# A planned order set anew: attention and a gated feed-forward on one core, with traced task durations in the planner

## The chip, the cores and the metric

One Trainium2 chip, one core in use. The metric is the device time of one launch in microseconds (us), the median of several runs. A profiled execution of the same kernel gives the trace; its own time is told beside its span.

## The reference

Block-sparse attention of 4 batches, 8 heads, 768 positions, head size 64, in blocks of 32 positions, followed by a feed-forward over the 3072 tokens:

```python
scores = scale * np.matmul(q, k.transpose(0, 1, 3, 2))
mask = np.abs(blk_i - blk_j) <= 1
mask = mask | (blk_i == 0) | (blk_j == 0) | (blk_i == n_blocks - 1) | (blk_j == n_blocks - 1)
...
mask[qb * block:(qb + 1) * block, kb * block:(kb + 1) * block] = True    # 3 sampled blocks per query block
scores = np.where(mask, scores, -1000000000.0)
attn = np.exp(scores - np.max(scores, axis=-1, keepdims=True))
attn = attn / (np.sum(attn, axis=-1, keepdims=True) + 1e-09)
x = np.matmul(attn, v)                    # regrouped to 3072 tokens x 512
h = x @ w_in                              # 512 x 2048
g = h * np.tanh(np.log1p(np.exp(h)))      # for h over 20 the logarithm is h itself
out = g @ w_out                           # 2048 x 512
```

The inputs q, k, v are float32, the weights float64 (the kernel reads them as pairs of int32).

## The kernel before

**The work.** Each batch is 13 attention jobs: 11 pairs of query blocks (a gathered set of 8 key blocks for each) and two dense rows of blocks (the first and the last, all 768 keys). A job makes scores `s` on TensorE (L774 for batch 0, in float32; L784 for the others, in float16 high and low parts), row maxima `mx` on VectorE (L827), exponentials `pt` on ScalarE (L853), turns them round (in batch 0 by TensorE transposes `t`, L873, copied to `pp` by ScalarE or VectorE; later by a transposing DMA), multiplies with v into `o` (L938, L954), scales to `xs`, transposes to `tx` and splits into `xh` and `xl` (L1038, L1040, L1043). Eight query blocks make one tile of 256 tokens. A tile then goes through the feed-forward: 16 pieces of 12 matmuls for h (L1228, "H pieces" below), a chain of elementwise work on `hs` and `us` (L1237 to L1275), and 16 pieces of 6 matmuls for the output y (L1289, "Y pieces"). There are 12 tiles, so 192 pieces of each kind.

**The start.** The float64 weights must be decoded on VectorE (L1078, L1081, L1084: 8 pieces of w_in, 16 of w_out), scaled by a root of a Gram matrix that TensorE makes (L475, reduced through `tp`, L501), and split into high and low halves (`wt`, `wi`, `wo` on GpSimd, ScalarE or VectorE). Until that is done for the first pieces there is no H piece to run, and TensorE fills waits that the planner foresees with multiplications by zeros (L1057).

**What sets the order.** Nothing is ordered by hand. `Plan.add` records some thousands of tasks, each with one or more engines that can do it ("ways"), a planned duration on each, a latency `lat`, buffers of rings, and a number `K(name, n)` out of the table `PRIO`. `Plan.emit` walks a planned time: at each step it takes, over all engines, the task with the earliest planned start, and within 0.02 us the one with the least `ready + key`; a task with several ways goes to the engine where it is planned to end first. The instructions are written out in that order, and each engine runs its own in order on the chip:

```python
late, bias = pace(t, start) if eng == "PE" else (0.0, 0.0)
cand.append((start + late, t.ready + t.key + bias, t.n, start, t, took))
...
c = min((c[1:] for c in cand if c[0] <= lo + 0.02), key=lambda c: c[:2])
...
self.zeros(int((idle - 0.3) / (0.25 if start > 15.0 else 0.4)))
```

The last line puts zeros into a planned wait of TensorE, between 3 and 150 us of planned time. `pace` ranks attention jobs on TensorE by `START` (planned times for the first 18 jobs) and `RES` (how much feed-forward is kept back behind the last job). So a duration or a number in the table can move any task on any engine, and can give it to another engine.

**Two places the prediction speaks of.** `gather_k` (L698 on GpSimd, L700 on ScalarE) copies three sampled key blocks into `kg` for a query block. `sums` (L551, its instruction at L466) squares and adds a loaded tile on ScalarE; `add_root` has TensorE add the result over the partitions (`tp`), in order with everything else on TensorE.

Of the kernel before, what the change touches and what calls it, by code (L numbers as in the profile page):

```python
# [114 lines left out]
    "gh": (359.8, 691.9, 379.7, -99.7),  # L115
    "gl": (401.7, 134.8, 711.4, 354.1),
    "ys": (-152.2, 277.9, -237.6, -376.8),
    "out": (274.8, 328.6, 274.4, -199.6),
}


# [1392 lines left out]
```

## Time and profile before

| | us |
|---|---|
| median of 3 runs | 715.48 (714.74 to 716.0) |
| the profiled execution, its own time | 715.61 |
| its span, first to last instruction | 713.8 |
| TensorE busy | 677.6 |
| VectorE busy | 561.5 |
| ScalarE busy | 533.75 |
| GpSimd busy | 255.9 |

The engines are named PE (TensorE matmul), PEld (its weight loads), DVE (VectorE), ACT (ScalarE), POOL (GpSimd) and SP (the queue that issues the DMAs). "Busy" is the time in which at least one instruction of the engine ran; a group's mean is of single instructions, which overlap a little on their engine. Idle time of PE is what the span has over its busy time; the zeros are busy but do no work.

### The profile page before, as it was taken

How to read it: one execution, taken by the hardware profiler on the slowest of the kernel's cores; microseconds unless marked ns; L12 is line 12 of the kernel's file. 1: busy time of each engine (PE TensorE's matmuls, PEld its weight loads, DVE VectorE, ACT ScalarE, POOL GpSimd, SP SyncE). 2: the span in 40 equal slices, each digit the busy share in tenths (PEclk: the TensorE clock that was granted, in tenths of full speed). 3: DMA queues.
4: the chain of work that ended last, by engine and by line, in shares of the span. 5: the costliest groups of instructions: out<-in, count | busy, mean ns of one | idle time of the engine just before them, and what ended most of it. 6: DMA issues, size and time to landing. Idle time of an engine off the chain costs nothing.

```text
span 713.8 us, 25374 instructions
## 1 busy us (share of the span) xinstructions
PE 677.6 (95%) x10342; PEld 448.4 (63%) x10342; DVE 561.5 (79%) x1052; ACT 533.7 (75%) x908; POOL 255.9 (36%) x339
## 2 busy tenths in 40 slices
PE   6878898799999999999999999999999999999997
PEld 2544576566667666666666666666666666666653
DVE  2798988999899887899998979989979778554250
ACT  1868768898898876879887886998878868555550
POOL 6547534982233441262235325435212123000000
PEclk9999999999999999999999999999999999999999
DMA  8978794556556775588665775885495565530000
GB/s 321 362 218 264 249 286 116 141 169 123 168 137 164 197 201 129 151 202 205 147 157 138 214 200 120 227 218 138 119 165 126 129 144 145 143 89 16 16 16 29
DMA packets 144599, 115.93 MB, mean 162 GB/s; under 512 B 96739, under 2 KB 107492, under 8 KB 144484
## 3 DMA queue, kind: packets, MB, share of 16 engines
q1 hardware_dynamic: 144480, 114.33, 59.8%
q8 instruction: 81, 1.33, 0.8%
q14 instruction: 34, 0.28, 0.1%
q10 hardware_dynamic: 4, 0.00, 0.0%
HBM read 79.32 MB, written 12.95 MB: 129 GB/s over the span
## 4 chain that ended last, share of the span: by engine, by line
PE 61%; DVE 16%; DMA 9%; ACT 6%; issue 4%; SPq 2%; POOL 1%; ACTq 0%; POOLq 0%; DVEq 0%
PE y L1289 27%; PE h L1228 25%; PE s L784 4%; PE o L954 4%; DMA wor<-in_moe_w_out_dram 2%; DMA vg<-vd 2%; DMA wr<-in_moe_w_in_dram 2%; DVE p L904 2%; DMA raw_q<-in_q_dram 2%; DVE mx L827 1%; ACT pt L853 1%; DVE hs L1262 1%; DVE kt L613 1%; DVE wo L1084 1%; SPq L734 1%
## 5 line engine op out<-in xcount | busy, mean ns | idle before, releaser
L1228 PE MATMUL h<-xh,wi 128*128 128x256 f16 x1536 | 284.6, 274 | 0.3 <-ACT xh L1038 0.3
L1289 PE MATMUL y<-wo,g 128*128 128x512 f16 x1152 | 278.6, 380 | 1.3 <-DVE ys L1302 0.9
L1228 PEld LDWEIGHTS <-wi 128*128 128x128 f16 x2304 | 222.3, 98 | 60.3 <-issue 5.9
L1228 PE MATMUL h<-xl,wi 128*128 128x256 f16 x768 | 210.2, 274 | 0.7 <-POOL xl L1043 0.7
L1289 PEld LDWEIGHTS <-g 128*128 128x128 f16 x1152 | 109.5, 98 | 105.6 <-issue 7.0
L698 POOL COPY kg<-kt 128x256 f16 (+1 forms) x132 | 65.6, 534 | 137.0 <-PE s L784 113.3
L853 ACT ACTIVATE pt<-s,nb,ns 128x256 f32<-128x256 f32 (+1 forms) x208 | 106.8, 578 | 3.9 <-DVE p L904 3.4
L1237 ACT ACTIVATE hs<-h 128x512 f32<-128x512 f32 x96 | 56.5, 589 | 50.3 <-PE h L1228 49.6
L1262 DVE SCALAR_TENSOR_TENSOR hs<-us,hs 128x1024 f32<-128x1024 f32 x48 | 62.5, 1301 | 22.4 <-ACT us L1261 22.2
L1040 POOL CAST xh<-tx 128x256 f16<-128x256 f32 (+1 forms) x39 | 27.5, 712 | 120.0 <-DVE tx L1020 119.8
L904 DVE SCALAR_TENSOR_TENSOR p<-pt,p 128x512 f16<-128x512 f32 (+1 forms) x102 | 64.2, 651 | 2.4 <-ACT p L897 2.1
L827 DVE TENSOR_REDUCE mx<-s 128x4 f32<-128x1024 f32 x44 | 53.3, 1212 | 7.0 <-PE s L784 5.9
L700 ACT ACTIVATE kg<-kt 128x256 f16 (+1 forms) x132 | 40.8, 372 | 23.3 <-DMA kt<-in_k_dram 11.6
L1252 ACT ACTIVATE us<-hs,hsc 128x1024 f32<-128x1024 f32 x48 | 55.1, 1148 | 1.0
L1260 ACT ACTIVATE us<-us 128x1024 f32<-128x1024 f32 x48 | 50.6, 1054 | 6.8 <-POOL us L1258 6.2
L1259 ACT ACTIVATE us<-us 128x1024 f32<-128x1024 f32 x36 | 38.0, 1055 | 18.6 <-DVE us L1256 18.4
L1261 ACT ACTIVATE us<-us 128x1024 f32<-128x1024 f32 x48 | 50.6, 1054 | 0.7
L1256 DVE TENSOR_SCALAR us<-us 128x1024 f32<-128x1024 f32 x48 | 34.9, 726 | 18.3 <-ACT us L1252 18.3
L1273 POOL TENSOR_TENSOR g<-hs,g 128x1024 f16<-128x1024 f32 x15 | 34.4, 2291 | 34.1 <-DVE g L1270 25.6
L1043 POOL TENSOR_TENSOR xl<-tx,xh 128x128 f16<-128x128 f32 (+1 forms) x41 | 31.9, 785 | 39.3 <-ACT xh L1038 31.0
L1275 DVE TENSOR_TENSOR g<-hs,g 128x1024 f16<-128x1024 f32 x33 | 42.0, 1274 | 2.3 <-ACT g L1268 1.9
L954 PEld LDWEIGHTS <-pp 128*32 128x32 f16 x2952 | 32.4, 97 | 12.3 <-issue 10.6
(207 smaller groups left out, 909.4 us busy)
## 6 DMA issues: line engine op xcount, KB each, us to landing
vg<-vd SPq DMA_DIRECT2D x304, 65.0 KB, 2.4
vg<-vd SPq DMA_DIRECT2D x80, 195.0 KB, 3.3
wr<-in_moe_w_in_dram SPq DMA_DIRECT2D x8, 1024.0 KB, 11.3
wor<-in_moe_w_out_dram SPq DMA_DIRECT2D x16, 512.0 KB, 7.2
vd<-v SPq DMA_DIRECT2D x12, 520.0 KB, 5.4
raw_v<-in_v_dram SPq DMA_DIRECT2D x12, 512.0 KB, 4.8
out_dram<-ys SPq DMA_DIRECT2D x24, 256.0 KB, 3.2
raw_k<-in_k_dram SPq DMA_DIRECT2D x9, 512.0 KB, 5.7
```

The source lines that it names most:

```text
L698: nc.gpsimd.tensor_copy(out=dst, in_=src)
L827: nc.vector.tensor_reduce(out=mx.rearrange("p g w -> p (g w)"), in_=tl[ks].rearrange("p g (w k) -> p (g w) k", k=KT), axis=AX.X, op=ALU.max)
L853: ex = lambda o, x, g, w: nc.scalar.activation(out=o, in_=x, func=AF.Exp, bias=nb[:, g, w:w + 1], scale=ns(w)[:, 0:1])
L904: nc.vector.scalar_tensor_tensor(out=x[:, 1, cs], in0=src, scalar=PSC, in1=x[:, 0, cs], op0=ALU.mult, op1=ALU.subtract)
L954: nc.tensor.matmul(o[cs, at] if v1 == VW else o[cs, at, 0:v1 - v0], p[:, k, g, cs], x, start=j == 0 and g == 0 and k == 0 and n == 0, stop ...
L1228: nc.tensor.matmul(h[:, f2].rearrange("p (s q) -> p s q", q=BS), wi[:, fp, w, cc, fs], x[:, :, cc], start=f2 == 0 and k == 0, stop=f2 == 1 ...
L1237: nc.scalar.activation(out=tl[kq][:, 2 * (fp % 2):2 * (fp % 2) + 2], in_=tl[kh], func=AF.Copy, scale=-2.0 * GSC)
L1252: nc.scalar.activation(out=us(), in_=hs(), func=AF.Exp, scale=hsc[:, b, k:k + 1])
L1260: add("ACT", 0.97, lambda: nc.scalar.activation(out=us(), in_=us(), func=AF.Ln, bias=1.0), w=[ku], key=K("ln", b))
L1261: add("ACT", 0.97, lambda: nc.scalar.activation(out=us(), in_=us(), func=AF.Exp, scale=-1.0), w=[ku], key=K("un", b))
L1262: add("DVE", 1.15, lambda: nc.vector.scalar_tensor_tensor(out=hs(), in0=us(), scalar=-0.5, in1=hs(), op0=ALU.add, op1=ALU.mult), r=[ku], w ...
L1289: nc.tensor.matmul(tl[ky], tl["g", b, t, k][:, g, f, q], wo[:, fc, w], start=fc == 0 and n == 0, stop=fc == NFC - 1 and n == 2)
```

## The change

The functions stay as they are. Changed are the planned durations of some kinds of task, all numbers of `PRIO`, and `RES` and `START`. The durations (planned us, old to new): Gram diagonal 0.4 to 0.45; `gather k` on POOL 1.0 to 1.5 in batch 0 and 1.3 to 1.35 later, on ACT 0.85 to 0.65 and 1.15 to 0.95; `gather v` latency 1.8 to 1.3 and transfer 1.1 to 0.9; the transposing DMA latency 1.8 to 1.2 and transfer 1.75 to 0.7; `xh` on POOL 0.4/0.65 to 0.65/0.75; `xl` on POOL 0.5/0.82 to 0.8/1.0; decode of w_in 1.15 to 1.2; `hs` 0.58 to 0.52; the exponential on `us` 1.06 to 1.13; the logarithm and the second exponential 0.97 to 1.03; `which` latency 3.6 to 4.2.

```diff
 PRIO = {
-    "zrow": (141.7, 556.6, 1317, -306.9),
+    "zrow": (565.9, 440.1, 1077, -454),
...
-        add("POOL", 1.0 if exact(b) else 1.3, lambda: fn("POOL"), r=KT3(b) + ["off"], w=[("kg", n)], use=[("kt", b)], port=2, key=K("gather k", b),
-            also=[("ACT", 0.85 if exact(b) else 1.15, lambda: fn("ACT"))])
+        add("POOL", 1.5 if exact(b) else 1.35, lambda: fn("POOL"), r=KT3(b) + ["off"], w=[("kg", n)], use=[("kt", b)], port=2, key=K("gather k", b),
+            also=[("ACT", 0.65 if exact(b) else 0.95, lambda: fn("ACT"))])
...
-            also=[("POOL", (0.4, 0.65)[n], lambda: xh_fn("POOL")), ("DVE", (0.2, 0.28)[n], lambda: xh_fn("DVE"))])
-        add("POOL", (0.5, 0.82)[n], lambda: xl_fn("POOL"), r=[("tx", i), ("xhw", i)], w=[("xw", i)], use=kx, key=K("xl", b),
+            also=[("POOL", (0.65, 0.75)[n], lambda: xh_fn("POOL")), ("DVE", (0.2, 0.28)[n], lambda: xh_fn("DVE"))])
+        add("POOL", (0.8, 1.0)[n], lambda: xl_fn("POOL"), r=[("tx", i), ("xhw", i)], w=[("xw", i)], use=kx, key=K("xl", b),
...
-    RES, START = 1075, [80.1, 3.3, 19.4, 700.3, 46.6, 28.7, 2.8, 317.9, 0, 87.8, 85.8, 90.6, 55.8, 91.2, 167.1, 137.8, 0, 174.3]
+    RES, START = 246.9, [0, 0.8, 141.1, 12.6, 47.6, 23.8, 63.3, 45.2, 0, 5.6, 51.6, 139.5, 80.5, 115.4, 106.4, 73.3, 20.3, 169.3]
```

What the new order moves shows at three places.

POOL in the start, before: between two scalings and splits of w_in pieces (`wt_i`, L1134, and `wi`, L1142) POOL makes gathers of batch 0 (`kg`, each three copies with a table read ahead).

```order
L1142 TENSOR_TENSOR wi<-wt_i_455,wi 128x1024
L1043 TENSOR_TENSOR xl_0_550<-tx_513,xh_0_549 128x128
L677 TENSOR_LOAD offk
L698 ISA
L698 COPY kg_113<-kt_134 128x4x32
...
L1134 TENSOR_SCALAR wt_i_728<-wi,ws_706 128x1024
L1142 TENSOR_TENSOR wi<-wt_i_728,wi 128x1024
L677 TENSOR_LOAD offk
...
L1142 TENSOR_TENSOR wi<-wt_i_731,wi 128x1024
```

And in the changed kernel:

```order
L1142 TENSOR_TENSOR wi<-wt_i_462,wi 128x1024
L1142 TENSOR_TENSOR wi<-wt_i_436,wi 128x1024
L1134 TENSOR_SCALAR wt_i_746<-wi,ws_718 128x1024
L1142 TENSOR_TENSOR wi<-wt_i_733,wi 128x1024
L1142 TENSOR_TENSOR wi<-wt_i_746,wi 128x1024
L1134 TENSOR_SCALAR wt_i_913<-wi,ws_894 128x1024
L1134 TENSOR_SCALAR wt_i_948<-wi,ws_894 128x1024
L1043 TENSOR_TENSOR xl_0_560<-tx_917,xh_0_559 128x256
```

The gathers have left POOL: of its 24 float32 copies 6 remain (two gathers), and ACT has 60 in place of 42.

PE at its first H piece (`h_0_0`), before: the last scores, transposes and Gram rows ahead of it.

```order
L774 MATMUL s_1484<-kt_134,q_1_176 32x96 x8
L774 MATMUL s_1484<-kg_112,q_1_176 32x160 x8
L774 MATMUL s_1484<-kt_134,q_2_845 32x96 x8
L774 MATMUL s_1484<-kg_113,q_2_845 32x160 x8
L873 MATMUL t_1_1530<-ident,pt_1430 128x128 x4
L938 MATMUL o_1558<-vg_114,pp_0_1259 32x65 x16
L475 LDWEIGHTS wo
L475 MATMUL gram_wo<-wo 128x128
...
L1228 LDWEIGHTS wi
L1228 MATMUL h_0_0_1603<-xh_0_549,wi 128x256
```

In the changed kernel:

```order
L774 MATMUL s_1379<-kg_113,q_1_174 32x160 x8
L873 MATMUL t_1_1420<-ident,pt_1339 128x128 x4
L475 LDWEIGHTS wo
L475 MATMUL gram_wo<-wo 128x128
...
L1057 LDWEIGHTS z_69
L1057 MATMUL zeros<-z_69 128x512
L938 MATMUL o_1464<-vg_114,pp_0_1196 32x65 x16
L1228 LDWEIGHTS wi
L1228 MATMUL h_0_0_1497<-xh_0_559,wi 128x256
```

One job's scores (32 matmuls of the program), one group of transposes and two groups of `gram_wo` (8 matmuls) that stood ahead of the first H piece now stand behind it; the zeros are 106 in all, from 112.

ACT at the squares of the second q tile of batch 1 (`raw_q_1_1`, L466), on which PE's `tp_q_1_1` waits, before:

```order
L853 ACTIVATE pt_14_3279<-s_14_3154,nb_14_3252,ns_1_0_2094 128x256 x4
L1237 ACTIVATE hs_0_1_2_3212<-h_0_1_5_3219 128x512
L1252 ACTIVATE us_0_1_2_3394<-hs_0_1_2_3212,hsc_84 128x1024
L466 ACTIVATE I-3405_3406,ss_q_1_1_3404<-raw_q_1_1_3243 128x1024
L897 ACTIVATE p16_14_1_3423<-pt_14_3279 128x512
```

And in the changed kernel:

```order
L853 ACTIVATE pt_14_3316<-s_14_3209,nb_14_3314,ns_1_0_2352 128x256 x2
L1237 ACTIVATE hs_0_1_3_3330<-h_0_1_7_3299 128x512
L1252 ACTIVATE us_0_1_3_3389<-hs_0_1_3_3330,hsc_84 128x1024
L1268 ACTIVATE g_0_1_2_3404<-hs_0_1_2_2845 128x1024
L897 ACTIVATE p16_14_1_3414<-pt_14_3316 128x512
L1237 ACTIVATE hs_0_2_0_3417<-h_0_2_0_3364 128x512
L466 ACTIVATE I-3518_3519,ss_q_1_1_3517<-raw_q_1_1_3380 128x1024
```

The same squares stand behind more feed-forward: 291 of ACT's compute instructions come up to them and with them, from 251, and on PE the wait `tp_q_1_1` has 34 H and 16 Y pieces ahead of it, from 29 and 11, with the same attention (scores up to job 14, outputs up to job 13).

## Rows read from the trace of the kernel before

**Rows 1.** Busy time of each engine by stretch; columns us, PE, PEld, DVE, ACT, POOL, PEclk, DMA share, GB/s.

```profile
0.00:24.00 24.00, 17.91 (x154) 7.27 (x155) 9.91 (x11) 5.97 (x12) 14.77 (x45) 0.93 0.94 341
24.00:87.00 63.00, 50.82 (x1052) 31.82 (x1050) 54.76 (x97) 48.51 (x118) 38.32 (x36) 0.97 0.83 256
87.00:111.00 24.00, 19.75 (x310) 16.09 (x310) 20.81 (x36) 15.91 (x31) 9.35 (x8) 0.96 0.85 265
111.00:184.00 73.00, 66.59 (x1139) 46.99 (x1138) 67.85 (x131) 66.28 (x108) 45.73 (x50) 0.97 0.57 149
184.00:690.00 506.00, 503.16 (x7606) 337.64 (x7604) 404.89 (x778) 392.53 (x639) 147.69 (x202) 1.00 0.58 145
690.00:713.80 23.80, 19.41 (x90) 8.60 (x88) 3.23 (x4) 4.54 (x5) 0.00 (x0) 0.99 0.09 33
sum 713.80, PE 677.63 PEld 448.41 DVE 561.45 ACT 533.75 POOL 255.85; mean PE 112.94 PEld 74.73 DVE 93.58 ACT 88.96 POOL 42.64
```

**Rows 2.** Groups by line and shape, PE: busy us, mean ns, idle before.

```profile
L1057 PE MATMUL zeros<-z 128*128 128x512 f16 x112 | 31.1, 424 | 1.1 <-POOL z L331 1.1
```

**Rows 3.** Waits of PE over the span: us in total, times, longest.

```profile
PE gram_wi L475 <- DVE wi L1084: 6.7, 4, 4.7
PE o L938 <- DMA vg<-vd: 4.1, 6, 2.9
```

**Rows 4.** Timeline of PE: start, us, what, idle before and its releaser.

```profile
83.92 0.40 PE L774 MATMUL s<-kt,q 64*32 64x96 f32 x16
...
85.06 0.66 PE L873 MATMUL t<-ident,pt 128*128 128x128 f32 x4
...
87.10 0.27 PE L1228 MATMUL h<-xh,wi 128*128 128x256 f16 x1 [0.26 <-ACT xh L1038]
...
183.19 0.38 PE L501 MATMUL tp_q<-ss_q,ones 128*128 128x1 f32 x2 [1.41 <-ACT I-3405_3406 L466]
```

**Rows 5.** The chain that ended last, 108 to 116 us: start, us, what.

```profile
110.74 2.22 PE h L1228 x12
112.97 0.23 PE gram_wo L475 x4
113.19 1.31 PE h L1228 x12
```

**Rows 6.** Groups by line and shape, ACT.

```profile
L853 ACT ACTIVATE pt<-s,nb,ns 128x256 f32<-128x256 f32 x192 | 95.7, 562 | 3.8 <-DVE p L904 3.4
L1237 ACT ACTIVATE hs<-h 128x512 f32<-128x512 f32 x96 | 56.5, 589 | 50.3 <-PE h L1228 49.6
L1259 ACT ACTIVATE us<-us 128x1024 f32<-128x1024 f32 x36 | 38.0, 1055 | 18.6 <-DVE us L1256 18.4
L700 ACT ACTIVATE kg<-kt 128x128 f32 x42 | 10.0, 303 | 13.9 <-DMA kt<-in_k_dram 11.6 <-issue 1.2 <-PE s L774 0.9
L1132 ACT ACTIVATE wt_i<-wi,ws 128x1024 f32<-128x1024 f32 x4 | 4.6, 1146 | 0.0
L995 ACT ACTIVATE xs<-o,r 128x64 f32<-128x64 f32 x18 | 4.3, 321 | 1.4 <-DVE r L974 1.4
```

**Rows 7.** Waits of ACT from 24 to 184 us, the longest in total.

```profile
ACT nb L840 <- DVE mx L827: 7.1, 6, 2.7
```

**Rows 8.** Groups by line and shape, DVE.

```profile
L827 DVE TENSOR_REDUCE mx<-s 128x4 f32<-128x1024 f32 x44 | 53.3, 1212 | 7.0 <-PE s L784 5.9 <-PE s L774 0.9
L1084 DVE SCALAR_TENSOR_TENSOR wo<-wor,wo 128x512 int32<-128x512 int32 x16 | 12.7, 806 | 0.0
```

**Rows 9.** Groups by line and shape, POOL.

```profile
L698 POOL COPY kg<-kt 128x128 f32 x24 | 13.8, 610 | 17.9 <-PE s L774 17.9
```

**Rows 10.** Timeline of DVE and POOL: a decode step alone, and one beside POOL.

```profile
10.49 1.22 DVE L1081 SCALAR_TENSOR_TENSOR wi<-wr,wi 128x1024 int32<-128x1024 int32 x1
...
44.86 1.48 POOL L1134 TENSOR_SCALAR wt_i<-wi,ws 128x1024 f32<-128x1024 f32 x1 [1.29 <-DVE ws L354]
45.40 2.02 DVE L1081 SCALAR_TENSOR_TENSOR wi<-wr,wi 128x1024 int32<-128x1024 int32 x1
```

More of the change, by code (lines that the diff above doesn't have):

```diff
@@ L113 @@
-    "un": (-125.9, 689.8, -657.5, 14.5),
-    "hm": (-13.9, 169.5, -232.1, 243.5),
[L115 to L118, printed above, removed]
+    "zrow": (565.9, 440.1, 1077, -454),
+    "zeros": (-979.7,),
+    "load32 k": (-494.8,),
+    "load32 q": (-868.2, -154.4, 142.2),
+    "load v": (-330.6, -203.9, -188.4, -137.9),
+    "which": (-78.8,),
+    "table": (132.1,),
+    "globals": (73.2, 998.9, -1292, -199.5),
[16 rows of a table added]
@@ new lines @@
+    "gsc": (716.2,),
+    "open": (463.2,),
+    "s": (-1195, 555.5, -581.2, 296.8),
+    "mx": (303.8, -598.3, -116.9, -1027),
+    "nb": (-932.6, -458.8, 524.2, -312.9),
+    "ex": (-154, -310.2, -176.8, 233.4),
+    "t": (-1125, 16),
+    "pp": (-910.5,),
+    "o": (535, -666.1, -458, -302.6),
+    "rc": (74.3,),
+    "xs": (-115.3, -223.8, 115.4, -699),
+    "tx": (-1055, -698.2, 25.9, -441.7),
+    "xh": (-114, 661.6, -677.8, 1005),
+    "xl": (-723.2, 463.1, -29, -752.2),
+    "gather k": (1230, 728.6, 1632, 901.4),
@@ new lines @@
+    "gather v": (431.4, 488.9, -22.9, 462, -683.1, -88, -368.2, -1132, -634.1, 655.9, 613.3, 513.8, -1053,
+        214.2, -60.8, 345.9, -541.9, 838.8, 80.6, -542.8, -789.8, -898.1, -12, -269.3, -307, -164.7),
+    "load wo": (-175.8, 195.4, -562.8, 304.8),
+    "decode wor": (-733.7, 232.3, 7.5, -367.1),
+    "gram wo": (-380.7,),
+    "diag wo": (-221.7,),
+    "rootp wo": (-722.2,),
+    "root wo": (112.5,),
+    "wo t": (-988.8, -667.1, -1535, -1081),
+    "wo hi": (3.7, -222.5, -721.4, -1016),
@@ new lines @@
+    "lo q": (-79, 39.1, -138.5, -317.9),
+    "clear": (-725.8,),
+    "dense v": (-772.9, -259.2, -151.7, -972),
+    "sc v": (4, 177.3, 1265, 39.6),
+    "ends": (13, 812.2, 854, 1427),
+    "hi v": (52, -744.9, 288.1, 423.8),
+    "lo v": (-79, -634.2, -185.6, 783.7),
+    "hsc": (19.5, 901.4, 154.7, 819.5),
+    "osc": (-176.8, -1712, 501.3, -1107),
+    "h16": (17, 577.8, 596, 1007),
+    "l16": (-40, -331.9, -446.3, 1),
+    "tdma": (-60, 715.8, 463.2, 506.9),
+    "xc": (1, 953.1, 1343, 1008),
@@ L119 @@
+    "kw": (8, 1186, 1147, 337.2),
+    "hs": (39, -343.6, -108, -7.1),
+    "us": (-514.6, -90.1, -43.8, -397.4),
+    "us1": (-527.1, 271.1, 161.7, -304.1),
+    "us2": (898, 275.6, -534.1, 1144),
+    "ln": (-873.2, 163.1, -576.3, -601.9),
+    "un": (124.3, 111.3, -266.9, -715.9),
+    "hm": (-353.6, 557.3, 300.2, 423.8),
+    "gh": (-65.7, 941.6, -49.3, -1234),
+    "gl": (486.7, 640.4, 1291, 698.3),
+    "ys": (-213.2, 64.4, 39.8, 126.1),
+    "out": (676.3, 574.9, 372.6, 765.5),
 }
@@ L491, in diag @@
                                            accum_out=out())
-        add("DVE", 0.4, diag, r=[kg], w=w, new=new_, key=K("diag " + key[0], n0))
+        add("DVE", 0.45, diag, r=[kg], w=w, new=new_, key=K("diag " + key[0], n0))
     def root_pe(key, ss, apart):
@@ L1238, in hs_fn @@
                                  scale=-2.0 * GSC)
-        add("ACT", 0.58, hs_fn, r=[kh], w=[("hsw", b, t, fp)],
+        add("ACT", 0.52, hs_fn, r=[kh], w=[("hsw", b, t, fp)],
             new=[("hs", kq)] if fp % 2 == 0 else (), use=[kq], key=K("hs", b))
@@ L1350, in attn_mish_kernel @@
     add("ACT", 1.0, lambda: which(new), w=["kq", "z"],
-        new=[("hs", ("z",))], key=K("which", 0), lat=3.6, kind=("dma", 0.0, 2))
+        new=[("hs", ("z",))], key=K("which", 0), lat=4.2, kind=("dma", 0.0, 2))
     add("POOL", 6.0, table, r=["kq"], w=["off"], use=[("z",)], key=K("table", 0))
```

93 lines of the change are left out of this document (21 added, 72 removed), and 32 rows, old and new, of the table PRIO.

## The prediction

> **What bounds the kernel now.** I read the busy times by stretch first [rows 1]. TensorE (PE) is busy for 677.6 of 713.8 us, so it idles for 36.2; the zeros, which are no work, take another 31.1 [rows 2]. What is left, some 646.5 us, is the work itself, and the change leaves every matmul of it in place. So the new time is 646.5 plus zeros plus idle time, and the question is only how much of those 67 us the new order gives back. The stretches tell where they lie. Up to 87 us, where the first H piece runs [rows 4], PE is busy for 68.7: 18.3 idle, and all zeros are there too. From 87 to 184 us it idles for 24.0 - 19.75 + 73.0 - 66.59 = 10.7, and that stretch ends on the longest late wait for ScalarE, at 183.2 us, where PE's `tp_q` waits 1.41 us for the squares of a q tile [rows 4]. From 184 to 690 us it idles for 2.8 in 506: there PE is full, and what the other engines do costs nothing as long as they keep up (DVE 80%, ACT 78% busy). The last 4.4 us are the last output's way out. So a gain must come from the first 184 us. There the helpers are the bound: from 111 to 184 us DVE is 93% and ACT 91% busy [rows 1], and PE's waits name both, and gathers by DMA [rows 3].
>
> **The change, part by part.** The work on each engine shifts little over the whole span: the same tasks, with some given to another engine. In the changed program POOL has 18 float32 gather copies fewer and ACT 18 more; a copy is 0.61 us on POOL [rows 9] and 10.0/42 = 0.24 on ACT [rows 6]. So the plan's old price for the gather on POOL (1.0 for three) was too low and its price on ACT (0.85) too high, and the new ones (1.5, 0.65) are nearer to these rows. From 184 us on I count every such move at nothing: it lies beside PE's 503 us of work; if that cover went, ACT would have to rise from 78% to full.
>
> *Up to the first H piece.* I count what each order puts ahead of it. On ACT two `wt_i` go (2.3 us), four `pt` (2.0), four `xs` (1.0) and a small one (0.3), and twelve gather copies come (2.9): 2.7 less [rows 6]. ACT was 77% busy from 24 to 87 us [rows 1], so at that share the first H piece comes 2.7/0.77 = 3.5 us earlier. On DVE nine decode steps of w_out go, at most 0.81 each, one row maximum of 1.21 and one copy of about 0.7, and two small instructions come [rows 8]: some 7 less, at its 87% share 8.1 us earlier. Both must be done; the ends are 3.5 and 8.1. ACT's longest wait there is for DVE's row maxima [rows 7], so DVE's relief reaches ACT in part, and I take the middle, 5.8. But PE also has less done by then: the scores of one job (83.92 to 85.06, 1.14 us), a group of transposes (0.6) [rows 4] and two Gram groups (0.23 each [rows 5]), 2.2 us that now come later. Net 3.6 (1.3 to 5.9).
>
> *From the first H piece to the `tp_q` wait.* PE did 97 - 10.7 = 86.3 us of work there. Now it has five H and five Y pieces more ahead of the wait, 10 x 1.31 [rows 5] (the Y pieces take about the same), and the 2.2 moved back: 101.6. ACT was busy for 82.2 [rows 1]. It gets 39 instructions more: three `hs` (1.8), eight passes over a whole tile for the exponentials, the squares and `g` (8.4 at 1.055 each), nine gather copies (2.5), eight `xs` (1.9), four `pt` (2.0), six halves of probabilities and `pp` (3.0), less an output (0.7) and with two small ones (0.7) [rows 6]: 19.6, so 101.8. The two are now equal: nothing is left over if ACT never idles. It will: I take the 91% that ACT reached from 111 to 184 us [rows 1], 101.8/0.91 = 111.9 us, so PE idles for 10.3 in place of 10.7. The ends are 85% (its mean over the whole stretch, 120.2 us, 18.6 idle, 7.9 lost) and 97% (104.9, 3.3 idle, 7.4 gained). I take 91% because that row is the stretch in which ACT was really loaded.
>
> *The rest.* Six zeros fewer save nothing by themselves: where PE must wait, a zero is only cover. After 184 us I leave the 2.8 and 4.4 us as they are; a new order can place one wait more or less, and the rows of the old one show waits of about 1 us there, so 0 to 3 us lost bounds it.
>
> The sum: 715.6 (the profiled execution's own time, 1.8 over its span) - 3.6 - 0.4 = 711.6 us. The median of the runs, 715.48, is 0.1 below that execution, and I give 711.5.
>
> **The clock.** Where PE stood still for some time, its granted clock shows dips: 0.93, 0.97, 0.96 and 0.97 in the four stretches up to 184 us, 1.00 after [rows 1]. An H piece after the 2.9 us wait for a gather took 2.22 us, and 1.31 at the full 2.4 GHz [rows 5]. So a long wait costs itself and some 0.9 us per piece behind it; that is in PE's busy time above, on both sides, and I keep it. The Trainium skill ("TensorE: Matmul & The Clock Gate", Part 1) says that an idle array falls to 1.2 GHz and activity releases it; the trace agrees with the two piece times, and by it a new order with longer single waits would lose one or two us more than its idle time.
>
> **The rivals.**
>
> *Slower: ACT becomes the bound.* The planner has moved gathers, passes and `xs` to ACT, and puts more feed-forward on it ahead of the squares that `tp_q` needs. If ACT only keeps its 85%, the second part loses 7.9, and with the 3.6 of the first the sum is 4.3 slower: 719.9. The point from which it decides: the second part may lose 3.6, so PE idle 14.3, stretch 115.9, ACT at 88%. For it speaks that 91% was reached only with POOL doing more; against it that ACT's waits were mostly for DVE [rows 7], which has less ahead of it here.
>
> *Nothing comes earlier.* The first 87 us move the same bytes at a DMA share of 0.94 and 0.83 [rows 1]. If transfers set the pace, the first H piece stays where it was, with 2.2 us less done before it: about 717, or 715.5 if PE fits that work into its waits. Against it: PE's waits name DVE and ACT more than DMA [rows 3].
>
> *A larger gain: DVE and POOL stop hindering each other.* A decode step takes 1.22 us alone and 2.02 beside a POOL instruction [rows 10]. If the gathers' move off POOL (18 x 0.61 = 11 us of POOL in the start) frees DVE so that it is never waited for, ACT runs at 97% and the first part gives 5.9: 715.5 - 5.9 - 7.4 = 702. The Trainium skill ("SBUF — State Buffer", Who interferes with whom) has it that a VectorE instruction with two SBUF inputs and a GpSimd instruction that reads SBUF shut each other out, while ScalarE waits on no one. The trace agrees with the 1.22 and 2.02. By that rule the move is a gain on DVE whatever ACT pays.
>
> **How the numbers follow.** A measurement of this kernel tells 0.2% (1.4 us) from no change. Chances: the forecast, 708 to 714, 0.42; the larger gain, 700 to 708, 0.15; about no change, 714 to 717, 0.15; slower through ACT or a wait moved, 717 to 725, 0.28. The likeliest is 711.5. The range takes in the ends of both parts short of their extremes, 703 to 720, and leaves out some 0.06 below and 0.1 above. Faster by over 0.2% (below 714.1) 0.57, within it 0.15, slower 0.28.
>
> **What would show it.** Right: zeros and PE's idle time up to the first H piece shrink, that piece starts near 81 us, and the second `tp_q` wait ends near 193 us with ten pieces more done. PE's busy time without zeros stays near 646.5, and after 200 us it idles for no more than some 5 us. The slower rival shows as ACT releasing PE's longest waits between 85 and 195 us, with ACT at 88% or less there. The larger gain shows as DVE's decode steps near 1.22 us throughout, and `tp_q` below 187 us. Wrong altogether would be a loss after 200 us, where I count nothing.

## The result, and the profile after

The changed kernel takes 723.95 us, the median of 4 runs (720.24 to 725.79), beside 715.11 (714.11 to 716.0) for the kernel before on the same chip. The ratio is 1.0107, with a 95% interval of 1.0077 to 1.0137: 1.1% slower. Ratios here and below are to runs of the kernel before on the same chip, without the few executions that were over 1.5% above the fastest of their kernel. The prediction was 711.5 with a range of 703 to 720, so the time lies outside the range and on the other side. The profiled execution took 725.79 us, with a span of 724.0.

The busy times by stretch, to be held against [rows 1] (columns as there):

```profile
0.00:24.00 24.00, 18.07 (x163) 8.20 (x163) 12.34 (x14) 8.59 (x21) 15.24 (x41) 0.86 0.94 351
24.00:87.00 63.00, 49.41 (x1034) 31.10 (x1035) 53.39 (x95) 47.91 (x124) 31.04 (x20) 0.97 0.82 248
87.00:111.00 24.00, 20.12 (x358) 16.32 (x359) 19.95 (x37) 16.29 (x38) 3.53 (x6) 0.93 0.85 244
111.00:184.00 73.00, 68.02 (x1024) 48.93 (x1023) 63.62 (x124) 68.35 (x112) 35.75 (x38) 0.98 0.46 127
184.00:690.00 506.00, 494.09 (x7608) 330.34 (x7606) 405.11 (x784) 396.71 (x643) 152.56 (x197) 1.00 0.64 150
...
194.00:690.00 496.00, 484.09 (x7454) 323.70 (x7454) 395.11 (x776) 387.15 (x630) 146.80 (x195) 1.00 0.64 148
690.00:725.00 35.00, 29.81 (x156) 15.05 (x154) 8.77 (x9) 9.95 (x11) 0.00 (x0) 0.99 0.06 23
```

Read the idle time of PE in them: 8.9 us from 87 to 184 (10.7 before), and 11.9 from 184 to 690 (2.8 before). The long middle, where I counted nothing, has lost 9.1. Two places of PE's timeline fix the border, the first H piece and the wait for the second q tile's squares (start, us, what):

```profile
81.86 0.28 PE L1228 MATMUL h<-xh,wi 128*128 128x256 f16 x1
...
194.03 0.28 PE L501 MATMUL tp_q<-ss_q,ones 128*128 128x1 f32 x2
```

Up to `tp_q`, which now waits for nothing, the kernel needs 194.0 - 183.2 = 10.8 us more and has ten pieces more done, 13.1 us of work: a gain of 2.3. From there to the end it needs 724.0 - 194.0 = 530.0 us, and needed 713.8 - 183.2 = 530.6 with those 13.1 us still to do: 12.5 lost. PE's busy time accounts for both parts of that loss. After `tp_q` it is 484.09 + 29.81 = 513.9; before, it was 503.16 + 19.41 and 0.8 ahead of 184 us, 523.4, or 510.3 without the ten pieces. So PE works 3.6 us longer on the same matmuls and idles for 8.9 more.

A second profiled execution of the same program (from the experiment "again, unmoved" below; its span is 720.0 us) has this `tp_q` at 189.38 us: 6.9 us gained up to it, 13.1 lost behind it. So the loss is steady between the two, and the gain ahead of it is not.

PE's waits from 184 us on, the longest groups (us in total, times, longest):

```profile
PE o L954 <- DMA vg<-vd: 2.3, 3, 1.2
PE y L1289 <- ACT ys L1300: 1.8, 2, 1.1
PE y L1289 <- DVE ys L1302: 1.8, 1, 1.8
PE tp_q L501 <- ACT I-6943_6944 L466: 1.2, 1, 1.2
PE tp_q L501 <- ACT I-10509_10510 L466: 1.1, 1, 1.1
```

There is no single releaser: gathers of v by DMA, both engines that copy outputs, and squares. What they have in common shows only on a queue that I had not read, SP's, which issues the DMAs. Its waits for PE's outputs `o` to free a gather's buffer (L728) are its slack: as long as SP waits for PE there, the gathers are ahead. First the kernel before, from 184 to 690 us:

```profile
SPq L728 <- PE o L954: 42.3, 24, 3.3
```

And the changed kernel:

```profile
SPq L728 <- PE o L954: 9.2, 7, 2.4
```

The slack has gone from 42.3 us to 9.2. Two places where it runs out are to be seen in the timeline of SP in the changed kernel:

```profile
270.94 1.45 SPq L544 DMA_DIRECT2D raw_v<-in_v_dram  x3
272.49 0.41 SPq L1306 DMA_DIRECT2D out_dram<-ys  x1
272.94 7.89 SPq L908 DMA_TRANSPOSE pp<-p  x2
280.93 0.52 SPq L728 DMA_DIRECT2D vg<-vd  x1
...
287.61 2.61 SPq L908 DMA_TRANSPOSE pp<-p  x2
...
420.72 1.45 SPq L544 DMA_DIRECT2D raw_v<-in_v_dram  x3
422.27 5.97 SPq L908 DMA_TRANSPOSE pp<-p  x2
```

A pair of the transposing DMAs that turn probabilities round (L908) takes SP 2.61 us to issue, at 287.61. Behind a load of three tiles of 512 KB (`raw_v`; at the first place with the store of an output between) a pair takes 7.89 and 5.97, and everything behind it on SP is late. At the first place those are the gathers of the next job, and PE waits for them twice:

```profile
288.02 0.27 PE L954 MATMUL o<-vg,pp 128*32 128x130 f16 x8 [1.17 <-DMA vg<-vd]
289.10 0.46 PE L954 MATMUL o<-vg,pp 128*32 128x130 f16 x32 [0.80 <-DMA vg<-vd]
```

After these waits come ten microseconds in which PE never idles and runs at a lower granted clock, 0.83 (columns as in [rows 1]); that is where part of the 3.6 us of longer work lies in this execution. In the second one the clock stays at 1.00 behind these two waits, and is 0.84 from 480 to 490 us, behind a wait of 1.87 us. The stretch of the first:

```profile
290.00:300.00 10.00, 10.00 (x102) 6.30 (x86) 7.52 (x23) 8.15 (x16) 1.48 (x4) 0.83 0.68 160
```

At the second place it is the engines that stand still first. VectorE must wait with the next halves of probabilities until the transposing DMA has read the old ones, ScalarE waits for VectorE, the output's copy comes late, and PE waits for it (from 184 to 690 us VectorE waits 7.8 us and ScalarE 5.7 for transposing DMAs to have read, from 1.9 and 0.6 before):

```profile
430.86 0.43 DVE L899 TENSOR_SCALAR p<-pt 128x512 f16<-128x512 f32 x1 [1.25 <-DMA pp<-p]
...
432.97 0.78 ACT L853 ACTIVATE pt<-s,nb,ns 128x512 f32<-128x512 f32 x1 [2.09 <-DVE p L904]
...
434.18 0.74 DVE L1302 TENSOR_SCALAR ys<-y,osc 128x512 f32<-128x512 f32 x1
...
434.98 1.46 PE L1289 MATMUL y<-wo,g 128*128 128x512 f16 x6 [1.80 <-DVE ys L1302]
```

So one kind of event, a pair of transposing DMAs behind a large load, appears under several names in PE's waits. The theory from here on (A) is that this costs the kernel its time. The rivals: ScalarE is the bound, or VectorE, by the work that moved to them (B); GpSimd's long steps hold VectorE; or an order this tight loses in any case, so that a wait which is removed comes back elsewhere (C).

### The profile page after: what moved, and what is told of

It reads as the page before. It is cut to its first block, busy times and chain, and to the rows that moved or that the text cites. A ratio compares the mean times of both kernels' runs of the same rounds, so it can differ in the third digit from the quotient of the medians.

```text
span 724.0 us, 25409 instructions
## 1 busy us (share of the span) xinstructions
PE 679.5 (94%) x10336; PEld 449.9 (62%) x10336; DVE 563.2 (78%) x1058; ACT 547.8 (76%) x944; POOL 238.1 (33%) x300
## 4 chain that ended last, share of the span: by engine, by line
PE 54%; DMA 14%; DVE 11%; ACT 9%; SPq 5%; issue 4%; POOL 3%; ACTq 0%; POOLq 0%; DVEq 0%
PE y L1289 23%; PE h L1228 21%; DMA vg<-vd 5%; DMA wor<-in_moe_w_out_dram 4%; PE s L784 3%; PE o L954 3%; DMA pp<-p 2%; DMA raw_q<-in_q_dram 2%; ACT pt L853 2%; POOL wt L1177 1%; SPq L734 1%; DVE p L904 1%; DVE hs L1262 1%; DMA wr<-in_moe_w_in_dram 1%; DVE mx L827 1%
## 5 line engine op out<-in xcount | busy, mean ns | idle before, releaser
L698 POOL COPY kg<-kt 128x256 f16 (+1 forms) x114 | 57.6, 543 | 111.1 <-PE s L784 93.8
L904 DVE SCALAR_TENSOR_TENSOR p<-pt,p 128x512 f16<-128x512 f32 (+1 forms) x102 | 67.5, 683 | 8.4 <-ACT p L897 7.8
L1273 POOL TENSOR_TENSOR g<-hs,g 128x1024 f16<-128x1024 f32 x21 | 48.8, 2325 | 50.0 <-ACT g L1268 30.7
L700 ACT ACTIVATE kg<-kt 128x256 f16 (+1 forms) x150 | 44.5, 362 | 22.5 <-DMA kt<-in_k_dram 11.0
L1259 ACT ACTIVATE us<-us 128x1024 f32<-128x1024 f32 x44 | 46.4, 1054 | 17.1 <-DVE us L1256 17.0
L1260 ACT ACTIVATE us<-us 128x1024 f32<-128x1024 f32 x48 | 50.6, 1054 | 3.8 <-POOL us L1258 3.0
L1261 ACT ACTIVATE us<-us 128x1024 f32<-128x1024 f32 x48 | 50.6, 1055 | 0.6
L1040 POOL CAST xh<-tx 128x256 f16<-128x256 f32 (+1 forms) x28 | 19.8, 712 | 93.2 <-DVE tx L1020 88.9
L1043 POOL TENSOR_TENSOR xl<-tx,xh 128x256 f16<-128x256 f32 (+1 forms) x37 | 32.8, 892 | 40.0 <-ACT xh L1038 29.1
L1256 DVE TENSOR_SCALAR us<-us 128x1024 f32<-128x1024 f32 x48 | 37.1, 774 | 9.9 <-ACT us L1252 9.9
L954 PE MATMUL o<-vg,pp 128*32 128x65 f16 (+2 forms) x2568 | 33.9, 205 | 2.9 <-DMA vg<-vd 2.3
```

The lines of the kernel that those rows point to most:

```text
L698: nc.gpsimd.tensor_copy(out=dst, in_=src)
L904: nc.vector.scalar_tensor_tensor(out=x[:, 1, cs], in0=src, scalar=PSC, in1=x[:, 0, cs], op0=ALU.mult, op1=ALU.subtract)
L954: nc.tensor.matmul(o[cs, at] if v1 == VW else o[cs, at, 0:v1 - v0], p[:, k, g, cs], x, start=j == 0 and g == 0 and k == 0 and n == 0, stop ...
L1260: add("ACT", 1.03, lambda: nc.scalar.activation(out=us(), in_=us(), func=AF.Ln, bias=1.0), w=[ku], key=K("ln", b))
L1261: add("ACT", 1.03, lambda: nc.scalar.activation(out=us(), in_=us(), func=AF.Exp, scale=-1.0), w=[ku], key=K("un", b))
```

## The experiments

Most experiments replay the planner's order with a few tasks moved or given to another engine. In `Plan.emit` the walk only logs each task, and the instructions are issued afterwards; with empty tables this gives the same program. A move puts tasks, by number, ahead of another; `WAYS` overrides the engine.

```diff
-            fn()
+            self.log.append((t.n, t.ways[WAYS.get(t.n, t.eng)][1]))
...
+        for ns, to in MOVES:
+            xs = [x for n in ns for x in self.log if x[0] == n]
+            self.log = [x for x in self.log if x not in xs]
+            at = [x[0] for x in self.log].index(to)
+            self.log[at:at] = xs
+        for n, fn in self.log:
+            fn()
```

In those kernels the lines stand 9 or 10 further down (L917 or L918 for L908). All results together; PE's idle time is that of 184 to 690 us in the profiled execution:

| kernel | median us | ratio to before (95%) | PE idle |
|---|---|---|---|
| changed, again | 724.39 | 1.0109 (1.0077 to 1.0142) | 12.2 |
| four pairs put first | 717.96 | 1.0061 (1.0033 to 1.0089) | 10.9 |
| of these only the two at `raw_v` loads | 720.24 | 1.0052 (1.0021 to 1.0084) | 8.3 |
| three pairs put first, three q loads earlier | 718.23 | 1.0032 (1.0000 to 1.0064) | 8.6 |
| that, and pieces put into waits | 718.49 | 1.0029 (0.9999 to 1.0058) | 7.3 |
| three pairs, three loads, and subtractions off GpSimd | 720.68 | 1.0077 (1.0043 to 1.0112) | 8.2 |
| changed, work given back to GpSimd | 728.82 | 1.0215 (1.0174 to 1.0256) | 15.9 |
| changed, old price of the transposing DMA | 722.7 | 1.0144 (1.0088 to 1.0200) | 8.9 |
| a plan that knows the stall | 730.65 | 1.0215 (1.0176 to 1.0254) | 14.8 |
| before, two pairs put ahead of a gather, behind a load | 718.94 | 1.0066 (1.0046 to 1.0086) | 4.6 |
| before, gathers of batch 0 on ScalarE | 717.92 | 1.0034 (1.0008 to 1.0060) | 2.9 |
| before, subtractions off GpSimd | 713.43 | 0.9967 (0.9944 to 0.9990) | 1.7 |
| before, squares off GpSimd | 714.06 | 0.9982 (0.9958 to 1.0006) | 2.5 |
| before, both off GpSimd | 712.04 | 0.9956 (0.9931 to 0.9982) | 1.2 |
| that, and a pair ahead of a q load | 717.22 | 1.0037 (1.0010 to 1.0063) | 4.1 |

**The changed kernel, pairs ahead of loads.** A pair is two tasks. Each of the four goes ahead of what stood before it: a k load, a v load, stores, a v load.

```diff
+MOVES = [([711, 714], 744), ([770, 773], 803), ([889, 892], 817), ([1124, 1127], 1157)]
```

> The changed kernel with its own order, but at four places the pair of transposing DMAs (pp<-p) that stands right behind a load of three 512 KB tiles (k of batch 2, v of batch 2, v of batch 3) or behind two stores and an output (before the q tile at 332 us) is put ahead of it in SP's queue; nothing else moves. Theory A (the transposing DMAs stall SP's queue there, 3 to 5 us beyond their 1.3 us each pair, so the gathers behind them come late and PE waits after 200 us): SP's time in the transposing DMAs falls from 133 to about 120 us, PE's idle time from 184 to 690 us falls from 11.9 to about 6 us, and the time to 716 to 719 us. Theory B (ACT carries too much since gathers and passes moved to it): nothing changes, 722 to 726. Theory C (any order this tight loses, the wait only goes elsewhere): 720 to 724, the same idle time at other places.

The loss falls from 1.1% to 0.6%, though the two intervals overlap, and PE idles for 10.9 us, far from the 6 that A gave. PE's waits for gathers go from 2.3 us to 1.0; in their place one move has made a new wait, since the k load that it delayed is now late:

```profile
PE tp_k L510 <- DVE ss_k L592: 1.4, 1, 1.4
```

**The kernel before, pairs put right behind loads.** The same theory from the other side: two pairs that stood behind a large load and the gathers after it are issued one gather earlier, so that a gather now waits for load and pair. The load is `raw_v` at the first place, right ahead of the pair, and `raw_k` at the second, with an output and a gather between. Nothing else moves.

```diff
+MOVES = [([734, 737], 703), ([1088, 1091], 1057)]
```

> The kernel before with its own order, but at two places (near 254 and 404 us) the pair of transposing DMAs is put right behind a load of three 512 KB tiles (at the second one with a gather between) and ahead of the second gather of the pair, as in the changed kernel. Theory A: the two pairs take 3 to 5 us longer, the gather behind them lands 5 to 8 us later than before, PE waits 1 to 3 us at each place; 717 to 721 us. Theories B and C: within 1 us of before, as SP waits for PE there anyway.

It costs 0.66% (0.46 to 0.86). SP's timeline has the stall, and PE's the same two waits for gathers as in the changed kernel:

```profile
250.06 1.45 SPq L553 DMA_DIRECT2D raw_v<-in_v_dram  x3
251.61 5.43 SPq L917 DMA_TRANSPOSE pp<-p  x2
...
405.27 4.96 SPq L917 DMA_TRANSPOSE pp<-p  x2
...
261.48 0.27 PE L963 MATMUL o<-vg,pp 128*32 128x130 f16 x8 [1.12 <-DMA vg<-vd]
262.51 0.46 PE L963 MATMUL o<-vg,pp 128*32 128x130 f16 x32 [0.76 <-DMA vg<-vd]
```

So two places, four instructions, bring the change's waits and more than half its size into a kernel whose order is otherwise the old one. Not all of it is the stall, though. At the first place the gather now issues 7.0 us after the load (257.09 - 250.06) and did so after 1.7 (254.41 - 252.70): of the 5.3 us between, 2.6 are what a pair takes in any case, and 2.8 are the stall. This run does not part the two.

**The changed kernel, work given back to GpSimd.** Seven gathers of batch 0 and eleven squares (L1258) go from ScalarE back to GpSimd; if ScalarE were the bound, this would gain.

```diff
+WAYS = {130: 'POOL', 281: 'POOL', 321: 'POOL', 342: 'POOL', 399: 'POOL', 421: 'POOL', 441: 'POOL', 1579: 'POOL', ...
```

> The changed kernel with its own order, but the seven gathers of batch 0 (three copies each) and the eleven squares of us that the change took from GpSimd to ScalarE are given back to GpSimd, each at its place in the program. Theory B: ACT is relieved by about 7 x 0.9 + 11 x 1.05 = 18 us, its waits go, 716 to 720 us. Theory A: the late waits stay, since SP's queue is as it was; 722 to 727, or more where GpSimd (1.9 us for a square) is slower than ScalarE and hinders DVE.

It loses another 1.1%. ScalarE does 10 us less from 184 to 690 us, and VectorE, which was given nothing, is busy for 8.5 more:

```profile
184.00:690.00 506.00, 490.09 (x7584) 327.29 (x7582) 413.61 (x781) 386.30 (x632) 175.88 (x206) 1.00 0.65 150
```

So relieving ScalarE at this price gains nothing: GpSimd's work costs VectorE time.

**The changed kernel with one old price.** Of the new durations those of one task are put back, the transposing DMA's, and the order is planned anew.

```diff
-            add("SP", 1.33, ..., lat=1.2, kind=("dma", 0.7, 1))
+            add("SP", 1.35, ..., lat=1.8, kind=("dma", 1.75, 1))
```

> The changed kernel with the planned price of the transposing DMA alone as before (1.35, latency 1.8, transfer 1.75); the plan sets the order anew: the same up to 177 us, another one behind it, in which loads of three tiles still stand ahead of pairs of transposing DMAs at two or three places. Theory A in its narrow form (the price of the transposing DMA put it behind the loads): 716 to 720. Theory A in its wide form (a pair behind a load stalls SP whatever the plan's price): 719 to 725, with the stalls at the new places. Theory B: as the changed kernel, 722 to 726.

The ratio is 1.0144, and its interval overlaps that of the changed kernel. SP stalls here too, at other places (6.40 us for a pair behind `raw_k`, 6.62 behind `raw_v`). That the new price alone had put pairs behind loads (716 to 720 us) is not borne out; beyond that the run tells little, as any new price makes another order, and where pairs and loads meet in it is left to chance.

**The changed kernel again, unmoved.** The replay with empty tables, to stand beside the next two on the same chip.

> The changed kernel with the same program on every engine, run beside the next three on the same chip, since the first round's comparison with it went over two sets of runs: 721 to 725 us. Theory A needs it to be slower than e5 and e6 by their amounts; if it comes out near 718, the first experiment showed nothing.

724.39 us in 12 runs, 1.0109: the replay itself costs nothing.

**Two pairs alone.** Only the two places shown above.

```diff
+MOVES = [([770, 773], 803), ([1124, 1127], 1157)]
```

> As the first experiment, but only the two pairs of transposing DMAs behind the loads of v (batches 2 and 3) are put ahead of them: the two longest stalls (5.3 and 4.5 us for one transposing DMA). Theory A: 2 to 4 us less than the changed kernel in this round, 719 to 722, and PE's waits near 288 and 435 us (1.2 + 0.8, 1.8) gone. Theory C (the wait only goes elsewhere): within 1 us of it.

1.0052, from 1.0109: moving four instructions of SP takes back half the loss (the intervals just touch; the medians of 12 runs each lie 4.2 us apart). The gathers have the same load and the same pair ahead of them as in the changed kernel, and each pair now takes 2.6 us, so here it is the stall that has gone. The waits near 288 and 435 us are gone too. SP's slack at L728 is 12.2 us, little more than the 9.2 before the move: it is not the slack in total that was regained.

**Three pairs, and three q loads earlier.** Where moving a pair ahead of a load would make the load late, the load itself is moved up.

```diff
+MOVES = [([669], 636), ([770, 773], 803), ([889, 892], 817), ([1023], 982), ([1124, 1127], 1157), ([1199], 1223)]
```

> As e5, with the pair behind the stores of v of batch 2 (near 327 us) put ahead too, and three loads of q tiles put one to four SP instructions earlier, where their buffers are free. Theory A, widened (SP's queue as a whole runs late after 200 us, so the q tiles land late as well, and PE's waits for their squares, tp_q, are of the same kind): 4 to 7 us less than the changed kernel in this round, 716 to 720, and the tp_q waits (0.5 to 1.2 us, five of them) shrink. If the squares wait for ScalarE rather than for the load, the tp_q waits stay and it is as e5.

1.0032 (1.0000 to 1.0064), an interval that lies wholly below that of the changed kernel: about two thirds of the loss. What the third pair and the loads add to the two pairs alone is not clear of noise. The pair that took 7.89 us at 272.94 now takes 2.62:

```profile
269.97 2.62 SPq L917 DMA_TRANSPOSE pp<-p  x2
272.64 1.60 SPq L553 DMA_DIRECT2D raw_v<-in_v_dram  x3
```

Three waits for squares remain (1.4, 1.2 and 1.0 us), against the expectation, and PE idles for 8.6 us, against 2.8 before. ScalarE's timeline tells what they are:

```profile
223.93 0.30 ACT L849 ACTIVATE nb<-mx,ns 128x4 f32<-128x4 f32 x1 [3.51 <-DVE mx L836]
...
225.18 1.05 ACT L475 ACTIVATE I-4357_4358<-raw_q 128x1024 fp8e4<-128x1024 f32 x1
...
311.89 1.04 ACT L475 ACTIVATE I-6478_6479<-raw_q 128x1024 fp8e4<-128x1024 f32 x1
...
333.27 1.06 ACT L475 ACTIVATE I-6943_6944<-raw_q 128x1024 fp8e4<-128x1024 f32 x1 [2.21 <-DMA raw_q<-in_q_dram]
```

Only the third waits for its load. The first two do not, and ScalarE comes to them late: it has waited 3.51 us for row maxima that stand ahead of the first, and works without a wait from 299 us, feed-forward for the most part, up to the second. So these two are B's kind of wait, by the order on ScalarE, and not A's.

**The kernel before, gathers of batch 0 on ScalarE.** The part of the change that the larger-gain rival rested on, done alone.

```diff
+WAYS = {130: 'ACT', 281: 'ACT', 321: 'ACT', 342: 'ACT', 399: 'ACT', 421: 'ACT', 441: 'ACT'}
```

> The kernel before with its own order, but the seven gathers of batch 0 that the change took from GpSimd are given to ScalarE, each at its place. The rival of the prediction (DVE and GpSimd hinder each other, the gathers' move frees DVE): 2 to 5 us faster than before, with DVE's decode steps nearer 1.22 us. If the first 200 us gained by the order alone: within 1.5 us of before, or 1 to 3 us slower, as ScalarE gets 7 x 0.9 us more ahead of the first H piece.

0.34% slower, and the first H piece comes at 89.26 us, not 87.10 [rows 4]. VectorE's decode steps come no nearer to 1.22 us: those of w_in at L1091 take 1.65 in the mean, and took 1.49 before (L1081 there). Alone, the move off GpSimd gains nothing.

**Pieces put into waits.** Onto the last but one: nine of PE's waiting instructions get the next H or Y piece ahead of them, to see if the rest is only the order of PE's own work.

> As e6, and at nine places after 200 us at which TensorE waited in the traces of the changed kernel, of e5 or of e6 (for the squares of a q tile, a gather, a copied output) the next piece of the feed-forward is put ahead of the waiting instruction. Theory A says that what is lost after 200 us is the sum of such waits, so it falls with them: 2 to 4 us less than e6's 718.2, 714 to 717. If the order loses in any case (theory C), the waits show up at other places and it stays at 717 to 720.

1.0029, the same as without. The waits for squares near 226, 313 and 334 us are gone, that for ScalarE's copy of y near 243 has doubled (1.12 to 2.28 us), and others of 0.7 and 0.8 come elsewhere. What is short is not work for PE at the right place; this is as C has it.

**A plan that knows the stall.** In the planner, a transposing DMA holds SP until the one before has moved, gathers are dearer, the transposing DMA's latency is 1.8 again, and the table is searched anew.

```diff
+                if len(t.kind) > 3:
+                    end = max(end, self.prev_t + 0.6)
...
-            key=K("gather v", su["ng"] if b == 0 else SUS + b), lat=1.3,
+            key=K("gather v", su["ng"] if b == 0 else SUS + b), lat=2.0,
```

> The changed kernel's durations of the engines, but the plan takes the gathers dearer (latency 2.0, transfer 1.1) and lets a transposing DMA hold SP's queue until the one before it has been moved, as the traces show; the numbers of the table, START and RES are searched anew under these prices, so the order is another one from the first instruction. Theory A (it was the prices of SP's queue that the order was tuned to): PE idles for under 6 us after 200 us, SP waits for PE's outputs again, the stalls of transposing DMAs over 2 us are fewer; 712 to 718 us. If the loss lies in the engines' new durations or in planning tightly at all: 718 to 726.

1.0215, as slow as the slowest of the others and outside both ranges expected. SP has its slack again, 43.0 us at this line, and no transposing DMA takes longer than 2.44 us; still PE idles for 14.8 us, now for squares (up to 2.4 us) and output copies:

```profile
184.00:690.00 506.00, 491.20 (x7590) 327.94 (x7589) 408.18 (x789) 388.55 (x643) 150.62 (x188) 1.00 0.61 149
```

So A in the wide form, that SP's queue alone makes an order good, falls. The order is new from the first instruction on, and the search was short, so this run does not say which of its places is at fault.

**Subtractions off GpSimd, changed kernel.** On the kernel with three pairs and three loads moved, the 21 subtractions that GpSimd makes for `g` (L1273) go to VectorE.

> As e6, and the 21 subtractions for the low half of g that the changed kernel's plan gives to GpSimd (2.3 us each) are done by VectorE (1.23 us), each at its place. If what is left of the loss comes from VectorE standing still beside GpSimd (a step of 0.77 us took 2.68 beside such a subtraction at 229 us, and PE waited for VectorE's and ScalarE's copies of y behind it): VectorE's busy time rises by less than half of the 21 x 1.23 = 26 us, the waits for copies of y near 243 and 457 us go, 714 to 717 us. If VectorE is simply short of time: its busy time rises by the full 26 us, 720 to 726.

No better: 1.0077, against both expectations in part, and the interval overlaps that of the kernel it started from. VectorE is not busier for it, 405.2 us for 407.4 from 184 to 690, although 21 instructions of some 1.25 us were added.

**The same in the kernel before.** Fifteen subtractions there, then eleven of its squares to ScalarE, then both.

```diff
+WAYS = {1584: 'DVE', 1642: 'DVE', 1774: 'DVE', 1850: 'DVE', ...
+WAYS = {..., 1579: 'ACT', 1621: 'ACT', 1713: 'ACT', ...
```

> The kernel before, its 15 subtractions for the low half of g on GpSimd done by VectorE, each at its place. By the same reasoning as e11: 1 us faster to 1 us slower, as PE idles for only 2.8 us after 184 us there; if VectorE is short of time, 2 to 6 us slower.

> The kernel before, eleven of its twelve squares of us on GpSimd (1.9 us) done by ScalarE (1.05 us), as the change has them, each at its place: one part of the change alone. Taking them back cost the changed kernel about 5 us. If that is GpSimd hindering VectorE, it helps here too, within what is to be had: 0 to 2 us faster. If ScalarE is short of time: 1 to 4 us slower.

> The kernel before with both moves: its 15 subtractions for the low half of g done by VectorE and eleven of its twelve squares of us by ScalarE, each at its place. If what the first move gave (0.33 per cent) is VectorE no longer held up beside GpSimd, the second adds a part of its own 0.18 per cent: 711.5 to 713.5 us where before is 715.3, VectorE's busy time from 184 to 690 us near 400 us in place of 404.9. If the two gain the same microseconds, it is as e12, 0.996 to 0.998 of before.

The subtractions alone gain 0.33% (0.10 to 0.56), the squares alone nothing that can be told, and both together 0.44% (0.18 to 0.69): 712.04 us, less than either kernel. The squares alone relieve VectorE, which was given nothing, from 404.89 us to 398.29 in the long middle, and give ScalarE 7.3 us more; neither shows in the time. With both moves VectorE is busy for 398.68, as expected. Two of VectorE's groups, first in the kernel before (busy us, mean ns, idle before):

```profile
L1275 DVE TENSOR_TENSOR g<-hs,g 128x1024 f16<-128x1024 f32 x33 | 42.0, 1274 | 2.3 <-ACT g L1268 1.9
...
L704 DVE COPY kg<-kt 128x768 f16<-128x768 f16 x66 | 28.2, 443 | 0.0
```

and with the subtractions alone moved, together with the busy times of the long middle:

```profile
L1285 DVE TENSOR_TENSOR g<-hs,g 128x1024 f16<-128x1024 f32 x48 | 61.4, 1280 | 2.6 <-ACT g L1278 2.4
...
L714 DVE COPY kg<-kt 128x768 f16<-128x768 f16 x66 | 25.8, 407 | 0.0
...
184.00:690.00 506.00, 504.30 (x7610) 338.02 (x7609) 407.01 (x792) 392.98 (x640) 115.67 (x189) 1.00 0.60 146
```

The fifteen add 19.4 us to the first group, and all of VectorE's groups together rise by 1.8 over the span (614.6 to 616.4): the others have become 17.6 us shorter, a copy of `kg` 443 ns to 407 for example. Some of that lies in the start, where only two of the fifteen stand. In the middle the other thirteen add 17.0 us and VectorE's busy time rises by 2.1, from 404.89 [rows 1]: about 15 us is what GpSimd had cost it there.

**And one pair ahead of a q load.** In the last kernel a pair still stalls behind a single q load. It is put ahead.

```diff
+MOVES = [([1344, 1347], 1377)]
```

> As e14, and the one pair of transposing DMAs that stands behind a load in the kernel before too (near 519 us, 3.4 us for one of them, and PE waits 1.0 us for the squares at 523.9 us) is put ahead of that load. By theory A 0 to 1.5 us less than e14; if the q tile then lands later by the pair's 2.6 us, its squares are later too and nothing is gained.

By the two ratios it costs some 0.8% against the kernel it started from. First SP there:

```profile
514.39 0.42 SPq L554 DMA_DIRECT2D raw_q<-in_q_dram  x1
514.92 3.81 SPq L918 DMA_TRANSPOSE pp<-p  x2
```

and with the pair ahead, SP, PE's longest wait, and the twenty microseconds behind:

```profile
516.52 2.62 SPq L918 DMA_TRANSPOSE pp<-p  x2
519.19 0.58 SPq L554 DMA_DIRECT2D raw_q<-in_q_dram  x1
...
PE tp_q L511 <- ACT I-11719_11720 L476: 2.7, 1, 2.7
...
520.00:540.00 20.00, 17.31 (x329) 11.50 (x314) 14.48 (x32) 13.38 (x22) 4.19 (x10) 0.91 0.51 131
```

The pair is faster by 1.2 us, the load issues 2.7 us later behind the gather ahead of it (4.2 us after 515.02, and it was 1.4 after 512.96), its squares come late, and PE stands for 2.7 us and then has a granted clock of 0.91. So a stall of a pair is not a loss by itself. What decides is which of the two has someone waiting behind it.

## Why the prediction was wrong

**The bound of the start** was read rightly in its dates, and in part by luck. "That piece starts near 81 us": 81.86. "The second `tp_q` wait ends near 193 us with ten pieces more done": 194.03, with ten more. The gain up to there is 2.3 us where the sum had 4.0, and 6.9 in the second execution. The first piece comes 5.2 us earlier where the sum had 5.8, although VectorE has 4.1 us less to do before it and not 7, and ScalarE 2.2 and not 2.7. From there to `tp_q` PE idles for 10.3 us, the very figure of the forecast, but not by its mechanism: ScalarE is 88% busy (98.4 of 112.2 us) and not 91, and PE's longest waits there are for a gather by DMA (2.3 us) and for VectorE (2.1). Two readings were off. The stretch of 97 us ran to 184, and the wait in it ends at 183.2. And the decode step that [rows 10] shows as one alone was not alone: a step of GpSimd of 0.25 us took 1.11 beside it (the line is in the last section). The figure stands even so, since the step at 38.62 us takes 1.23 with GpSimd idle.

**"The rest"** is the step that failed: "After 184 us I leave the 2.8 and 4.4 us as they are", with "0 to 3 us lost" as its bound. The measured loss is 12.5 us, and the prediction had named it as what would show it wrong altogether. The reason given was that "what the other engines do costs nothing as long as they keep up (DVE 80%, ACT 78% busy)". Those shares hardly changed (405.11 and 396.71 us of 506, so 80% and 78%) and PE idles for four times as long. A share of busy time over 506 us says nothing on single dates. What the runs showed in its place: SP, whose queue carries the loads, the gathers and the transposing DMAs together, does not stand among the engines that I counted, and pairs of transposing DMAs that stall there behind large loads make about half of the loss. The planner's new price for a transposing DMA is the same whatever stands before it; the trace shows 2.61 us for one pair, and 5.97 and 7.89 for two others.

**The clock.** The prediction said that a new order with longer single waits would lose a microsecond or two more than its idle time. Here it is 3.6 us of longer work beside 8.9 of idle time (4.0 beside 9.2 in the second execution), with a granted clock of 0.83 behind the waits near 288 us. None of these waits in the middle is over 1.8 us (1.9 in the second execution); before, none was over 1.0.

**The rivals.** Slower through ScalarE gave 719.9 and had a chance of 0.28 with the cases like it; its side was right, and its mechanism was not at work where I put it. ScalarE is 94% busy from 111 to 184 us (68.35 of 73) without making `tp_q` wait, and giving work back to GpSimd makes the kernel slower. Later in the kernel squares do stand late on ScalarE, as two of the three waits left by the moved pairs and loads show. Nothing comes earlier: refuted by 81.86. The larger gain: the gathers alone off GpSimd give no gain in the kernel before, so its mechanism did not work where I put it. It works elsewhere: long GpSimd steps in the feed-forward do hold VectorE, by the 15 us above. And that a measurement tells 0.2% from no change was too fine: the intervals here reach 0.2 to 0.6% to either side.

**What is shown and what stays open.** Shown: two pairs of transposing DMAs that stall behind large loads make half of the changed kernel's loss, since with the same gathers behind them and no stall it is gone. In the kernel before, two pairs put ahead of a gather, behind such loads, cost 0.66%, by their place and the stall together. With a third pair and three loads of q moved, two thirds are taken back, of which the last part is not clear of noise. Open: the last third, with the head start (2.3 us in one execution, 6.9 in the other) that should have made it faster. It is not the place of PE's pieces, nor the subtractions on GpSimd; that SP's dates alone do not settle it is shown by the plan that knows the stall. Of the waits left, two for squares are ScalarE's own order; what they cost was not tried by itself, and the waits for output copies were not separated further.

## What to carry to other kernels

Read the queue that issues the DMAs as an engine, and its waits for a consumer to free a buffer as the places where it has time. Read them place by place: in total they told where to look here (42 us to 9), but the kernel before lost 0.66% to two pairs with 37 us of them left, and the plan with 43 us was among the slowest. The kernel before also has a stall of 4.91 us, behind two loads of 520 KB at 450 us, for which PE does not wait at all. A planned duration that is a median holds only where the neighbours are the usual ones; before trusting a new order, look in it for what stands right behind each large load, and ask of both who waits for them. And where an engine is nearly full, an instruction that another engine could make may be cheap on it, if it frees it from a neighbour that holds it up.
